# Two ranks of a planner changed in the opening of an attention and mixing kernel: evacuations of batch 0's token units, value products of batch 1

## The chip, the cores and the metric

The kernel runs on one core of a Trainium2 chip. TensorE (PE) multiplies matrices into PSUM banks, VectorE (DVE), ScalarE (ACT) and GpSimd (POOL) work on elements, and SyncE (SP) issues the DMAs between HBM and SBUF. Each engine works through its own instructions in order and waits for others by semaphores. The metric is the device time in microseconds (us).

## The reference

Eight batches, eight heads, 576 positions, head size 64. Attention is windowed: four heads see the last 32 positions, four see every fourth of the last 128. Its output, as rows of 512 channels, is the input x of a second part.

```python
scores = np.where(masks, scale * q @ k.T, -1e9)
attn = exp(scores - max); attn = attn / (sum(attn) + 1e-9)
x = attn @ v                                  # per batch 576 x 512
theta = x @ w_theta
zr, zi = x * cos(theta), x * sin(theta)
y = w_tok_r @ zr + w_tok_i @ zi               # mixes positions
u = x + y
out = u + maximum(u @ w_ch, 0)
```

All is float32. The kernel splits each operand of the large products into a high and a low part and adds three products (high by high, high by low, low by high).

## The kernel before, in words

A batch is done in stages. Heads go in four pairs. `scores` puts a pair's scores into two PSUM banks (tag s, two buffers), adds the mask there by a product with an identity matrix for batch 0 and a few pairs of batches 1 and 2, takes the maxima (L430, DVE), scales them (L438, DVE), lets ACT do the exponentials with their sums (L485) and normalises on POOL (L510). `turn` transposes the probabilities P in eight pieces on DVE (L525) into one of two buffers pt. `pv` multiplies them with the values (L617, tile o), ACT copies the result to x (`x_evac`, L581), and `x_split` makes high and low parts (xh: L593 on ACT, L597 and L599 on DVE, for the last pair on POOL). `theta` multiplies x with w_theta (L685), `trig` makes sines and cosines, and `zsplit` the parts zh and zl. A batch has 16 units of 288 columns: eight `token` units y (27 matmuls, L850, over the nine z tiles in the order of `KORD`) and eight `chan` units c (12 matmuls, L882). A token unit ends in `residual`, which adds it to x (L825, DVE), makes u's high part (L828, ACT) and low part (L830, POOL) and so frees the bank; a channel unit ends in `finish` (L859).

Units of batch b run on PE while batch b+1 goes through attention. The weights come as packed words and are unpacked once, in the opening: clamp (L332, DVE), two steps on ACT (L334, L340), join (L342, DVE), high part (L350, ACT), low part (L352, POOL). The token weights of the second half of the positions (`late_wt_a`, `late_wt_b`) and the channel weights (`late_wc`) come late; a channel weight is loaded into the staging space that an earlier weight leaves when its L352 is done (`LATE2`), and x_split of batch 1 then takes the same spaces.

The order in the opening (batch 0, and batch 1 up to its theta) is dealt out by a small planner, `Order`. Every piece of work is a generator that names an engine and an estimate. `run` picks the engine that can start first, and on it, among the pieces ready by its estimates, the one with the lowest rank:

```python
t = min((t for t in ready if t[4] == eng and t[2] <= at), key=lambda t: (t[0], t[1]))
```

A piece that starts another without a rank hands its own on, so x_evac and x_split of batch 1 run at the rank of their `pv`. `residual` and `finish` are started with a rank of their own, RANK["evacuate"] (L853, L884). Loads have RANK["load"]. The order found is the order of the program; on the chip nothing is reordered. From batch 1's own units on (`phase`) the order is written out by hand and the ranks play no part.

Of the kernel before, what the change touches and what calls it, by code (L numbers as in the profile page):

```python
# [30 lines left out]
LATE = ("u3", "xh1", "xh2", "xh3", "xh0")  # L31
LATE2 = ("xh2", "xh3", "xh2", "xh3")
RANK = dict(load=6.64, scores0=1.09, flip=0.01, pv0=1.13, pair=.21, theta_unpack=1.54, theta0=5.3, trig0=2.41,
            token_early=2.55, theta_split=6.42, token_late=6.75, chan=2.1, units=2.95, evacuate=4.49,
            scores1=4.02, scores2=7.3, pv1=8.0, theta1=5.96, trig1=7.42)
STS = (4, 0, 1, 2, 3)


# [1020 lines left out]
```

## Time and profile before

| | |
|---|---|
| median of 3 runs | 577.86 us (577.52 to 578.83) |
| profiled execution | 577.82 us, of it span 576.0 us |
| mean granted clock of PE | 0.988 |
| busy PE / DVE / ACT / POOL | 550.5 / 378.0 / 345.2 / 222.2 us |
| moved by DMA | 81.91 MB, mean 142 GB/s |

A row of the timeline gives start and length in us, engine, line, operation, tiles, how many instructions it holds, and in brackets the idle time before them with what ended it. A matmul's end is modelled: starts are what to go by. The granted clock of PE is 1.00 at 2.4 GHz and 0.50 at 1.2 GHz; a value between is a mean.

### The profile page before, as it was taken

The page shows a single profiled execution, that of the slowest core. Times are in us where ns is not written, and L with a number is a line of the kernel's source. Part 1 is how long each engine was busy: PE and PEld are TensorE (multiplying, and loading weights), DVE is VectorE, ACT ScalarE, POOL GpSimd, SP SyncE. Part 2 cuts the span into 40 slices and gives each one's busy share as a digit, 9 for nine tenths or more (in the row PEclk, how much of TensorE's full clock was granted, in tenths as well). Part 3 has the DMA queues.
Part 4 walks back from the last instruction along what each step waited for, and adds up shares of the span by engine and source line. Part 5 has one row for each costly group of instructions (what it writes and reads, how often), then busy time and mean ns, then how long its engine had stood idle before and what let it go on. Part 6 is the DMA issues. An engine that isn't in the chain of part 4 may idle for free.

```text
span 576.0 us, 13996 instructions
## 1 busy us (share of the span) xinstructions
PE 550.5 (96%) x5464; PEld 501.6 (87%) x5464; DVE 378.0 (66%) x1156; ACT 345.2 (60%) x939; POOL 222.2 (39%) x206
## 2 busy tenths in 40 slices
PE   5997799999999999999999999999999999999997
PEld 4744688879999899988999899988999899989997
DVE  3879798865666668756776768756775767445112
ACT  1498967768555784369555785359556695266110
POOL 2228855525224352226324253226323353325220
PEclk9999699899999999999999999999999999999999
DMA  8991437601747046540746146550747123321002
GB/s 303 400 368 28 165 105 245 216 0 63 231 150 193 32 162 210 169 127 20 268 143 172 64 148 202 181 136 11 252 146 190 69 83 102 77 89 65 18 1 83
DMA packets 45586, 81.91 MB, mean 142 GB/s; under 512 B 3920, under 2 KB 19024, under 8 KB 45520
## 3 DMA queue, kind: packets, MB, share of 16 engines
q1 hardware_dynamic: 45520, 81.02, 43.7%
q8 instruction: 43, 0.70, 0.5%
q14 instruction: 23, 0.19, 0.1%
HBM read 64.49 MB, written 16.52 MB: 141 GB/s over the span
## 4 chain that ended last, share of the span: by engine, by line
DVE 34%; ACT 30%; PE 25%; issue 5%; POOL 2%; DMA 2%; SPq 0%; ACTq 0%; POOLq 0%; DVEq 0%
DVE pt L525 16%; PE y L850 11%; ACT P L504 11%; PE c L882 6%; PE th L685 3%; DVE P L409 3%; ACT K L698 3%; ACT K L787 3%; DVE xh L599 3%; ACT th L796 2%; ACT zh L644 2%; DVE xq L729 2%; DVE K L789 2%; ACT cos L705 2%; ACT x L581 2%
## 5 line engine op out<-in xcount | busy, mean ns | idle before, releaser
L830 POOL TENSOR_TENSOR u<-x,u 128x288 fp32r<-128x288 f32 x64 | 54.7, 858 | 184.6 <-ACT u L828 184.6
L525 DVE STREAM_TRANSPOSE pt<-P 32x288 f32<-32x288 f32 x224 | 105.1, 469 | 12.0 <-POOL P L510 8.9
L882 PE MATMUL c<-u,late_wc 128*128 128x288 f32 x768 | 110.2, 296 | 2.8 <-DVE x L859 2.8
L882 PEld LDWEIGHTS c<-u,late_wc 128*128 128x128 f32 x768 | 106.0, 188 | 6.8 <-DVE x L859 4.0
L850 PE MATMUL y<-wtkh,zh 128*128 128x288 f32 x288 | 90.3, 314 | 1.1 <-ACT zh L644 1.1
L850 PE MATMUL y<-wtkh,zl 128*128 128x288 f32 x288 | 86.2, 299 | 4.0 <-POOL zl L646 4.0
L646 POOL TENSOR_TENSOR zl<-g,zh 128x512 fp32r<-128x512 f32 x40 | 52.3, 1316 | 97.5 <-ACT zh L644 84.5
L504 ACT ACTIVATE P<-P,mx 128x64 f32<-128x64 f32 x216 | 72.0, 335 | 25.8 <-DVE mx L498 25.8
L850 PE MATMUL y<-wtkl,zh 128*128 128x288 f32 x288 | 85.9, 298 | 0.0
L828 ACT CAST u<-x 128x288 fp32r<-128x288 f32 x64 | 26.9, 429 | 86.2 <-DVE x L825 85.5
L685 PE MATMUL th<-wthh,xh 128*128 128x512 f32 x224 | 74.8, 395 | 0.3 <-DVE g L784 0.3
L850 PE MATMUL y<-late_wt_b,zh 128*128 128x288 f32 x320 | 68.1, 297 | 0.0
L825 DVE TENSOR_TENSOR x<-y,x 128x288 f32<-128x288 f32 x64 | 28.1, 448 | 53.6 <-PE y L850 53.5
L850 PEld LDWEIGHTS y<-wtkh,zl 128*128 128x128 f32 x288 | 55.1, 191 | 4.7 <-POOL zl L646 4.7
L850 PEld LDWEIGHTS y<-wtkh,zh 128*128 128x128 f32 x288 | 54.9, 191 | 4.7 <-ACT zh L644 2.3
L850 PE MATMUL y<-late_wt_a,zh 128*128 128x288 f32 x256 | 56.3, 301 | 0.0
L850 PEld LDWEIGHTS y<-wtkl,zh 128*128 128x128 f32 x288 | 55.1, 191 | 0.3 <-issue 0.3
L510 POOL TENSOR_TENSOR P<-P,sm 128x576 f32<-128x576 f32 x32 | 37.5, 1172 | 41.1 <-DVE sm L508 18.1
L850 PEld LDWEIGHTS y<-late_wt_b,zh 128*128 128x128 f32 x320 | 51.4, 189 | 0.3
L685 PEld LDWEIGHTS th<-wthh,xh 128*128 128x128 f32 x224 | 42.0, 188 | 9.2 <-DVE g L784 0.6
L850 PE MATMUL y<-late_wt_b,zl 128*128 128x288 f32 x160 | 47.4, 296 | 0.0
L581 ACT COPY x<-o 128x576 f32<-128x576 f32 x32 | 29.4, 919 | 28.4 <-PE o L617 19.1
(108 smaller groups left out, 1106.3 us busy)
## 6 DMA issues: line engine op xcount, KB each, us to landing
q<-in_qT_dram SPq DMA_DIRECT2D x32, 576.0 KB, 5.2
va<-in_vw_dram SPq DMA_DIRECT2D x30, 320.0 KB, 3.2
k<-in_kT_dram SPq DMA_DIRECT2D x28, 304.0 KB, 5.5
out_dram<-x SPq DMA_DIRECT2D x28, 288.0 KB, 2.4
vb<-in_vw_dram SPq DMA_DIRECT2D x29, 256.0 KB, 3.8
xd<-xq SPq DMA_DIRECT2D x24, 288.0 KB, 5.1
xn<-xd SPq DMA_DIRECT2D x24, 256.0 KB, 3.4
st_wtk<-in_wtk_dram SPq DMA_DIRECT2D x8, 576.0 KB, 8.8
```

Of the source, the lines that this page charges most:

```text
L409: pin(nc.vector.tensor_tensor_reduce(out=P[:, n], in0=ps[:, n - g0], in1=mskb[:, mask_of(pr, n)], op0=ALU.add, op1=ALU.max, scale=1.0, sca ...
L504: table(nc.scalar.activation(P[:, n], P[:, n], AF.Exp, bias=mx[:, n:n + 1], scale=SCALE, accum_out=sm[:, n:n + 1]))
L510: pin(nc.gpsimd.tensor_tensor(P, P, sm.unsqueeze(2).to_broadcast([128, NJ, BW]), op=ALU.mult))
L525: pin(nc.vector.transpose(pmats[b, pr][k0:k0 + QB, :, hh, QB * e:QB * e + QB], P[p0:p0 + QB, :, QB * o:QB * o + QB]))
L581: pin(nc.scalar.copy(dst, src))
L646: pin(nc.gpsimd.tensor_tensor(lo, z, hi.bitcast(F32), op=ALU.subtract))
L685: pe(nc.tensor.matmul(pt, l, r, start=(n == 0), stop=(n == 3 * NC - 1)))
L825: pin(nc.vector.tensor_tensor(x[:, ts], ps, x[:, ts], op=ALU.add))
L828: pin(nc.scalar.copy(uh[b, d][:, ts], x[:, ts]))
L830: pin(nc.gpsimd.tensor_tensor(ul[b, d][:, ts], x[:, ts], uh[b, d][:, ts].bitcast(F32), op=ALU.subtract))
L850: pe(nc.tensor.matmul(ps, l[:, cs], r, start=(n == 0), stop=(n == 3 * NK - 1)))
L882: pe(nc.tensor.matmul(ps, l[:, cs], r[:, ts], start=(n == 0), stop=(n == 3 * NC - 1)))
```

## The change

The rank of evacuations falls from 4.49 to 1.49: below sines and cosines (2.41 and 7.42), units (2.95), channel weights (2.1) and all scores after batch 0's. The rank of batch 1's value products falls from 8.0 (plus 0.21 per pair) to 5.0: below theta of batch 1 (5.96), the late token weights (6.75) and the scores of batch 2 (7.3).

```diff
--- before.py
+++ after.py
@@ -31,8 +31,8 @@
 LATE = ("u3", "xh1", "xh2", "xh3", "xh0")
 LATE2 = ("xh2", "xh3", "xh2", "xh3")
 RANK = dict(load=6.64, scores0=1.09, flip=0.01, pv0=1.13, pair=.21, theta_unpack=1.54, theta0=5.3, trig0=2.41,
-            token_early=2.55, theta_split=6.42, token_late=6.75, chan=2.1, units=2.95, evacuate=4.49,
-            scores1=4.02, scores2=7.3, pv1=8.0, theta1=5.96, trig1=7.42)
+            token_early=2.55, theta_split=6.42, token_late=6.75, chan=2.1, units=2.95, evacuate=1.49,
+            scores1=4.02, scores2=7.3, pv1=5.0, theta1=5.96, trig1=7.42)
 STS = (4, 0, 1, 2, 3)
 
 
```

No instruction is added or taken away. The order is the same on every engine up to the middle of token unit y0_2_0 of batch 0 (74 us in the trace), and again from early in the theta of batch 1 on. Names: y0_1_1 is batch 0's token unit for channels 128 to 255 and the second half of the positions, o1_3 the value product of batch 1's pair 3, s2_1_0 the first part of the scores of batch 2's pair 1, pt1 the turned probabilities that o1_3 reads.

PE where the value product of pair 3 stands, before:

```order
L850 MATMUL y0_2_1_1297<-late_wt_a_802,zh0_3_795 128x288 x2
L850 MATMUL y0_2_1_1297<-late_wt_a_802,zl0_3_796 128x288
L850 MATMUL y0_2_1_1297<-late_wt_b_1008,zh0_7_754 128x288 x2
L850 MATMUL y0_2_1_1297<-late_wt_b_1008,zl0_7_755 128x288
L617 MATMUL o1_3_1341<-pt1_109,va1_3_1110 64x64 x10
L617 MATMUL o1_3_1341<-pt1_109,vb1_3_1260 64x64 x8
L850 MATMUL y0_2_1_1297<-late_wt_b_1008,zh0_8_581 128x288 x2
L850 MATMUL y0_2_1_1297<-late_wt_b_1008,zl0_8_582 128x288
L850 MATMUL y0_3_1_1411<-late_wt_a_802,zh0_0_612 128x288 x2
L850 MATMUL y0_3_1_1411<-late_wt_a_802,zl0_0_613 128x288
```

It stood near the end of token unit y0_2_1, behind the scores of pair (2,1). The same product in the changed kernel:

```order
L850 MATMUL y0_1_1_1235<-late_wt_b_936,zh0_7_754 128x288 x2
L850 MATMUL y0_1_1_1235<-late_wt_b_936,zl0_7_755 128x288
L850 MATMUL y0_1_1_1235<-late_wt_b_936,zh0_8_581 128x288 x2
L850 MATMUL y0_1_1_1235<-late_wt_b_936,zl0_8_582 128x288
L617 MATMUL o1_3_1291<-pt1_109,va1_3_1124 64x64 x10
L617 MATMUL o1_3_1291<-pt1_109,vb1_3_1227 64x64 x8
L850 MATMUL y0_2_1_1302<-late_wt_a_802,zh0_0_612 128x288 x2
L850 MATMUL y0_2_1_1302<-late_wt_a_802,zl0_0_613 128x288
L850 MATMUL y0_2_1_1302<-late_wt_b_936,zh0_4_576 128x288 x2
L850 MATMUL y0_2_1_1302<-late_wt_b_936,zl0_4_577 128x288
L424 LDWEIGHTS idb_94
L424 MATMUL s2_1_0_1333<-mskb_93,idb_94 128x64
```

It now stands right behind token unit y0_1_1, ahead of all of y0_2_1 and of the scores of pair (2,1).

DVE around the turn of the pair that this product reads (the transposes into pt1), before:

```order
L597 TENSOR_TENSOR xh1_0_1133<-x1_0_903,xh1_0_1133 128x64
L525 STREAM_TRANSPOSE pt1_109<-P1_3_968 32x9x32 x2
L342 SCALAR_TENSOR_TENSOR st_wch1_1113<-st_wch1_1113 128x512
L525 STREAM_TRANSPOSE pt1_109<-P1_3_968 32x9x32 x2
L430 TENSOR_REDUCE mx2_0_1166<-s2_0_0_1168 128x5
L525 STREAM_TRANSPOSE pt1_109<-P1_3_968 32x9x32 x2
L438 TENSOR_SCALAR mx2_0_1166<-mx2_0_1166 128x5
L525 STREAM_TRANSPOSE pt1_109<-P1_3_968 32x9x32 x2
L430 TENSOR_REDUCE mx2_0_1166<-s2_0_5_1203 128x4
L599 TENSOR_TENSOR xh1_0_1133<-x1_0_903,xh1_0_1133 128x512
```

One join of a channel weight and the maxima of batch 2's first scores stood between the pieces. In the changed kernel:

```order
L599 TENSOR_TENSOR xh1_1_1162<-x1_1_1060,xh1_1_1162 128x512
L430 TENSOR_REDUCE mx2_0_1158<-s2_0_0_1160 128x5
L342 SCALAR_TENSOR_TENSOR st_wch1_1088<-st_wch1_1088 128x512
L525 STREAM_TRANSPOSE pt1_109<-P1_3_992 32x9x32 x2
L597 TENSOR_TENSOR xh1_0_1204<-x1_0_897,xh1_0_1204 128x64
L525 STREAM_TRANSPOSE pt1_109<-P1_3_992 32x9x32 x2
L825 TENSOR_TENSOR x0_0_274<-y0_0_1_1100,x0_0_274 128x288
L332 TENSOR_SCALAR st_wch2_1170<-st_wch2_1170 128x512
L525 STREAM_TRANSPOSE pt1_109<-P1_3_992 32x9x32 x2
L599 TENSOR_TENSOR xh1_0_1204<-x1_0_897,xh1_0_1204 128x512
L342 SCALAR_TENSOR_TENSOR st_wch2_1170<-st_wch2_1170 128x512
L525 STREAM_TRANSPOSE pt1_109<-P1_3_992 32x9x32 x2
```

The pieces now have the clamp and the join of the third channel weight, the parts of xh1_0 and an evacuation between them, and the scaling of the maxima comes behind the last.

POOL around the last piece of the late token weights (late_wt_b from st_wtk1_4), before:

```order
L510 TENSOR_TENSOR P1_2_905<-P1_2_905,sm1_2_907 128x576
L352 TENSOR_TENSOR late_wt_b_1008<-st_wtk1_3_479,late_wt_b_1008 128x576
L352 TENSOR_TENSOR late_wt_b_1008<-st_wtk1_4_698,late_wt_b_1008 128x288
L830 TENSOR_TENSOR u0_3_1121<-x0_3_476,u0_3_1121 128x288
L510 TENSOR_TENSOR P1_3_968<-P1_3_968,sm1_3_970 128x576
L830 TENSOR_TENSOR u0_0_831<-x0_0_274,u0_0_831 128x288
```

It followed the piece before it. In the changed kernel:

```order
L352 TENSOR_TENSOR late_wt_b_936<-st_wtk1_3_479,late_wt_b_936 128x576
L830 TENSOR_TENSOR u0_3_1101<-x0_3_476,u0_3_1101 128x288
L352 TENSOR_TENSOR late_wc0_1134<-st_wch0_961,late_wc0_1134 128x512
L510 TENSOR_TENSOR P1_3_992<-P1_3_992,sm1_3_994 128x576
L352 TENSOR_TENSOR late_wt_b_936<-st_wtk1_4_698,late_wt_b_936 128x288
L352 TENSOR_TENSOR late_wc1_1207<-st_wch1_1088,late_wc1_1207 128x512
```

An evacuation's low part, the first channel weight and the normalisation of P of pair 3 now stand in front of it.

## Rows read from the trace of the kernel before

**Rows 1.** Busy time of the engines, page, part 1.

```profile
PE 550.5 (96%) x5464; PEld 501.6 (87%) x5464; DVE 378.0 (66%) x1156; ACT 345.2 (60%) x939; POOL 222.2 (39%) x206
```

**Rows 2.** Windows: busy time of PE, PEld, DVE, ACT, POOL; PEclk, DMA, GB/s.

```profile
75.00:99.00 24.00, 22.95 (x331) 20.39 (x330) 21.43 (x48) 16.74 (x57) 12.97 (x12) 1.00 0.58 196
102.00:105.00 3.00, 3.00 (x28) 2.61 (x26) 2.19 (x8) 2.19 (x10) 1.25 (x1) 0.50 0.81 257
105.00:106.00 1.00, 1.00 (x10) 0.72 (x10) 0.61 (x3) 0.18 (x1) 0.00 (x0) 0.82 0.97 380
...
126.00:200.00 74.00, 74.00 (x709) 68.86 (x708) 48.31 (x162) 46.70 (x129) 27.83 (x26) 1.00 0.43 130
```

**Rows 3.** Timeline of PE: start, length, instruction, count, idle before it.

```profile
82.47 0.31 PE L424 MATMUL s<-mskb,idb 128*128 128x64 bf16 x5 [1.04 <-ACT P L485]
...
88.42 0.43 PE L850 MATMUL y<-late_wt_a,zh 128*128 128x288 f32 x2
88.68 0.30 PE L850 MATMUL y<-late_wt_a,zl 128*128 128x288 f32 x1
...
95.71 0.80 PE L617 MATMUL o<-pt,va 128*64 128x64 f32 x20
...
101.51 0.30 PE L424 MATMUL s<-mskb,idb 128*128 128x64 bf16 x2 [1.95 <-ACT P L485]
...
107.86 0.80 PE L617 MATMUL o<-pt,va 128*64 128x64 f32 x20
...
120.27 0.49 PE L685 MATMUL th<-wthh,xh 128*128 128x512 f32 x1 [0.33 <-DVE g L784]
...
125.11 0.63 PE L759 MATMUL xn<-idt,x 128*128 128x128 f32 x4 [1.02 <-DVE g L750]
```

**Rows 4.** Groups of DVE, 86 to 112 us: busy us, mean ns, idle before.

```profile
L525 DVE STREAM_TRANSPOSE pt<-P 32x288 f32<-32x288 f32 x22 | 10.3, 469 | 0.4
L342 DVE SCALAR_TENSOR_TENSOR st_wch<-st_wch 128x512 uint32<-128x512 uint32 x4 | 2.9, 736 | 0.1
L332 DVE TENSOR_SCALAR st_wch<-st_wch 128x512 f32<-128x512 f32 x4 | 2.3, 571 | 1.6 <-DMA st_wch<-in_wch_dram 1.5
L825 DVE TENSOR_TENSOR x<-y,x 128x288 f32<-128x288 f32 x4 | 1.8, 452 | 0.5 <-PE y L850 0.5
...
L599 DVE TENSOR_TENSOR xh<-x,xh 128x512 fp32r<-128x512 f32 x2 | 1.4, 691 | 0.0
...
L430 DVE TENSOR_REDUCE mx<-s 128x5 f32<-128x320 f32 x2 | 1.0, 493 | 0.1
...
L597 DVE TENSOR_TENSOR xh<-x,xh 128x64 fp32r<-128x64 f32 x2 | 0.4, 215 | 0.0
```

**Rows 5.** Timeline of DVE.

```profile
80.54 0.17 DVE L438 TENSOR_SCALAR mx<-mx 128x5 f32<-128x5 f32 x1
...
84.77 1.30 DVE L438 TENSOR_SCALAR mx<-mx 128x5 f32<-128x5 f32 x1
...
86.43 0.75 DVE L438 TENSOR_SCALAR mx<-mx 128x4 f32<-128x4 f32 x1
...
91.07 0.43 DVE L332 TENSOR_SCALAR st_wch<-st_wch 128x512 f32<-128x512 f32 x1
91.53 0.96 DVE L525 STREAM_TRANSPOSE pt<-P 32x288 f32<-32x288 f32 x2
```

**Rows 6.** Timeline of POOL.

```profile
84.60 1.45 POOL L352 TENSOR_TENSOR late_wt_b<-st_wtk,late_wt_b 128x576 fp32r<-128x576 f32 x1 [0.76 <-ACT late_wt_b L350]
86.00 1.15 POOL L510 TENSOR_TENSOR P<-P,sm 128x576 f32<-128x576 f32 x1
...
90.27 0.81 POOL L830 TENSOR_TENSOR u<-x,u 128x288 fp32r<-128x288 f32 x1 [0.94 <-ACT u L828]
```

**Rows 7.** Group of POOL, 72 to 118 us.

```profile
L352 POOL TENSOR_TENSOR late_wc<-st_wch,late_wc 128x512 fp32r<-128x512 f32 x4 | 5.5, 1385 | 2.6 <-ACT late_wc L350 2.6
```

**Rows 8.** DMA issues, 60 to 125 us: count, KB each, median us to landing.

```profile
vb<-in_vw_dram SPq DMA_DIRECT2D x4, 256.0 KB, 5.4
```

## The prediction

> **What bounds the kernel now.** I read the busy times of the page first: TensorE (PE) works 550.5 of 576.0 us [rows 1], so only time in which PE idles or runs at its lower clock can be won or lost. The windows [rows 2] then say where that is: from 126 us to 200 us PE is busy all the time at full clock. What the change moves lies between 74 and 143 us (the order of every engine is the same up to 74 us and, names apart, again from early in batch 1's theta on), so whatever delay PE has when this stretch ends goes into the time in full. The timeline of PE [rows 3] names the waits in it: 1.04 us before 82.47 and 1.95 us before 101.51 (both: a score bank held until ScalarE's exponentials are done), 0.33 at 120.27 and 1.02 at 125.11 (both: the theta chain on VectorE). After the idle 1.95 us the granted clock is 0.50, that is 1.2 GHz, for 102 to 105 and part of 105 to 106: a mean of 0.82 in that last us means 0.36 us at half. So 3.36 us at half clock, in which 1.68 us of work are lost [rows 2]. After the wait of 1.04 it stays at 2.4 GHz (1.00 over 75 to 99), and it is there again from 126 on [rows 2, 3]. Together PE loses 1.04 + 1.95 + 0.33 + 1.02 + 1.68 = 6.02 us. The change can win no more than that here.
>
> The profiled execution took 577.82 us, its span 576.0 with 1.8 around it; the median of the runs is 577.86, so the sum below is made on 577.8 and needs no shift. From about 0.2%, 1.2 us, a difference can be told from none.
>
> **The change part by part.** No instruction is added or removed (DVE's two more rows are runs that print apart); two ranks change, and the planner deals out a new order. Times below are on the clock of the trace.
>
> *First wait (82.47).* PE's score matmuls of pair (1,2) now come six token matmuls earlier. On VectorE the scaling of their maxima (L438) stands behind two transposes fewer (2 x 0.47) and one L342 more (0.74) [rows 4], so it ends 0.2 us earlier, and the exponentials behind it too. But PE comes to the bank three token matmuls sooner: the two of the row at 88.42 and the next begin 0.26 apart, so 0.13 each, 0.40 for three [rows 3]. The wait becomes 1.04 + 0.40 - 0.24 = 1.20. Unit y0_1 starts at 88.6 instead of 88.42.
>
> *Value product of pair 2 (o1_2) and the last late weights.* PE comes to o1_2 at about 92.9 instead of 95.71 [rows 3]: 24 y matmuls (3.2) and about half of batch 2's first scores with their masks (1.1: before, the 7.3 us from 88.42 to 95.71 held 39 y matmuls, 5.1, and all of them). It needs the turned P of pair 2. Before, that turn ended at 91.53 + 0.96 = 92.5 [rows 5]. Now one L342 more stands in front of its end (0.7), y0_3's evacuation no longer makes VectorE wait (0.5, the idle time of L825 in [rows 4]), and the scores come 0.1 sooner: 92.6. Bounds: 92.2, if VectorE is held less there than before, and 94.5 if the first channel weight's L332, now in front of the maxima of pair 3, is caught by GpSimd. What shows that price is L438 at 84.77: 1.30 us, ending with GpSimd's L352 (84.60 to 86.05), and at 86.43: 0.75 us, ending with the L510 after it; undisturbed such a scaling takes 0.17 (80.54 in [rows 5]). The weights themselves are no wait: their slot is free when GpSimd has done the first piece of late_wt_b, which now is at 80 (L342 ends near 77.8, cast and product take 2.1), and a load on this queue takes 5.4 us or less [rows 8], so it lands by 85.4, and VectorE comes to it near 84.7: what it may wait is inside the bounds.
> The last piece of late_wt_b is a new wait. On GpSimd it stood right behind its forerunners, and PE never waited for it; now u0_3 (0.8, at about 90.4; before at 90.27), a channel weight (1.39) and P of pair 3 (1.15) run ahead of it [rows 6, 7], and with its own 0.8 (half as long as the piece at 84.60) it is done at about 94.6. PE wants it after o1_2 (1.2 us), at 94.1: 0.5 us. Between 0 and 1.3.
>
> *Value product of pair 3 (o1_3), the main term.* Before it stood 24 y matmuls and the scores of pair (2,1) later, at 107.86 [rows 3]. Now PE comes to it right behind y1_1. The work up to there is what PE did before from 88.42 to 99.56 (101.51 less the idle 1.95) without a wait, less three y matmuls: 99.3 with the 0.16 from above, 99.8 with the 0.5.
> It needs the turn of pair 3 on VectorE, eight transposes. Between the turn of pair 2 and the end of this one the changed queue has two L332, two L342, two L597, two L599, one L430 and one L825 as well. At the means of the stretch [rows 4]: 8 x 0.469 + 2 x 0.571 + 2 x 0.736 + 2 x 0.215 + 2 x 0.691 + 0.493 + 0.452 = 9.1 us. From 92.6 that is 101.7, with GpSimd in the way no more than it is on average. Yet GpSimd now runs from 90.4 to 94.6 without a gap, and its product for the second channel weight starts when VectorE's L342 for the same weight ends, two transposes ahead of an L597: both times VectorE comes with an instruction of the kind that was held. Two holds cost (1.30 - 0.17) + (0.75 - 0.17) = 1.7 us at 84.77 and 86.43 [rows 5, 6]. I take these two: 103.4, a wait of 3.6 us. Bounds: 101.0 (turn of pair 2 at 92.2, L332 at its undisturbed 0.43 [rows 5], no hold) and 105.3 (94.5 + 9.1 + 1.7).
> On the price of a hold the Trainium skill speaks against this change: "SBUF — State Buffer", section "Who interferes with whom", has VectorE and GpSimd share a port pair which the one that issues first keeps for its whole instruction while the other "fully blocks", tensor_scalar and two-input VectorE instructions among them. The trace agrees (1.30 us, ending with GpSimd's 1.45). By that rule a third L597 hold would count in full as well, 0.8 more, and the sum would be 580.3; by the means alone it would be 577.7.
>
> *Clock.* The new wait is longer than the 1.95 us that took the clock to 1.2 GHz before. I price it as that one: 1.68 us. Bounds: 0, if the wait stays near the 1.04 that cost none, and 3.4, a stretch at half clock twice as long.
>
> *Theta.* The waits of 0.33 and 1.02 come from the addition L784, which stood behind eight transposes of pair (2,1); now it stands behind two, so much of them goes; but GpSimd's work for that pair also comes later. 0.75 remains, between 0 and 1.35.
>
> *Cover.* The other moved steps (casts on ScalarE, loads on SP's queue) are hidden by the wait before o1_3. The second half of pair 2's values is such a load: it follows o1_1 on the queue, so it is issued near 89.3, and took 5.4 us before [rows 8], with two channel weights close in front of it; now one of them runs 6 us sooner. It lands between 93 and 94.7, where o1_2 wants it at 93.5. What it adds there PE would wait at o1_3 otherwise. With that cover gone (A below) it costs up to 1.2 us.
>
> **Sum.** 1.20 + 0.5 + 3.6 + 1.68 + 0.75 = 7.7 against 6.0: 1.7 us more, 579.5 us. From 126 us on PE has no slack in which that could be given back [rows 2].
>
> **The rivals.**
> *A, faster: VectorE is in time and the clock holds.* Place: o1_3. Without a hold it starts at 101.0, PE came at 99.3, and a wait of 1.7, between the 1.04 that kept the clock and the 1.95 that lost it, may keep it. Loss 1.20 + 1.7 + 0.2 = 3.1, so 2.9 less than before: 574.9 (576.6 if the clock does fall). It decides at a start of about 101.9: with the clock lost, the sum is 6.0 there. For it: L332 on its own takes 0.43. Against: GpSimd has no gap there. 13%.
> *B, no difference.* Holds as in the mean, start at 101.7: 1.20 + 0.5 + 1.9 + 1.68 + 0.6 = 5.9, 577.7 us. For it: these means have holds in them already. With starts between 101 and 103 around it, 27%.
> *C, much slower.* The chain of maxima, exponentials and sums is held twice before the turn of pair 2, which ends at 94.5: o1_2 waits 1.6, o1_3 until 105.3 (PE there at 101.3: 4.0), and the clock is lost for twice as long: 1.20 + 1.6 + 0.4 + 4.0 + 3.4 + 0.75 = 11.4, 583.2 us. For it: L332 now comes to the port at the moment in which P of pair 2 is ready for GpSimd, 84.6. Against: the bank waits of batch 2's scores have 2 us of air. 15%.
> The forecast has 45%, with a range of its own from 578.5 to 581.5.
>
> **How the numbers follow.** Faster by over 0.2%: A, 13%. Within it: B, 27%. Slower: forecast and C, 60%. The range goes from 576.6 (most of A lies below) to 582.6 (most of C lies above).
>
> **What would show it.** In the changed trace PE should idle 3 to 4 us just before o1_3, near 100 to 103.5, put down to VectorE's transposes; the granted clock should be 0.50 after it; the wait before 101.51 for the scores of batch 2 should be gone, as they come later; the wait before 82.47 should still be there at 1.1 to 1.3. L332 and L597 near 93 and 98 should take about 1 us each. It is wrong if o1_3 starts before 102, if PE waits longest elsewhere, or if PE has idle time after 126 us that takes the delay up.

## The result, and the profile after

The changed kernel takes 579.53 us (median of 22 runs, 577.69 to 583.07), the kernel before 578.03 us beside it (22 runs, 575.68 to 579.68): ratio 1.0033, 95% interval 1.0021 to 1.0046. That is 1.5 us slower; 579.5 us and 1.7 more were predicted. The profiled execution of the change took 579.39 us, its span is 577.6.

Executions differ before the change has any say. So the two traces are compared from the last product of batch 0's token units that stands in front of every moved instruction; it is the last row at which the two timelines of PE still run alike, and is called the common product below. Before:

```profile
74.38 0.29 PE L850 MATMUL y<-wtkh,zl 128*128 128x288 f32 x1
```

After, the same product, and below it the waits of PE until theta, with the idle time in brackets:

```profile
74.09 0.29 PE L850 MATMUL y<-wtkh,zl 128*128 128x288 f32 x1
...
82.04 0.31 PE L424 MATMUL s<-mskb,idb 128*128 128x64 bf16 x5 [1.28 <-ACT P L485]
...
93.93 0.69 PE L617 MATMUL o<-pt,vb 128*64 128x64 f32 x16 [0.27 <-DMA vb<-in_vw_dram]
...
103.05 1.22 PE L617 MATMUL o<-pt,va 128*64 128x64 f32 x17 [3.20 <-DVE pt L525]
...
126.81 0.63 PE L759 MATMUL xn<-idt,x 128*128 128x128 f32 x4 [0.58 <-DVE g L750]
```

From the common product to the end of the span the kernel before needs 576.0 - 74.38 = 501.62 us, the change 577.6 - 74.09 = 503.51: 1.89 more. The waits answer to [rows 3]: 1.28 for 1.04 at the first bank, 0.58 in place of 0.33 and 1.02 in theta, no wait for batch 2's scores where there were 1.95, and 3.20 us before o1_3 (L617, put down to VectorE's transposes), which did not wait before.

Busy times change little; this row of the page answers to [rows 1]:

```profile
PE 551.3 (95%) x5464; PEld 502.7 (87%) x5464; DVE 379.5 (66%) x1156; ACT 345.3 (60%) x939; POOL 220.9 (38%) x206
```

The windows of the change (length, PE busy, PEclk, DMA share, GB/s) answer to [rows 2]:

```profile
99.00:102.00 3.00, 0.85 (x7) 0.94 0.86 303
102.00:105.00 3.00, 1.95 (x34) 0.50 0.08 31
105.00:108.00 3.00, 3.00 (x17) 0.50 0.62 197
108.00:110.00 2.00, 2.00 (x28) 0.88 0.00 0
110.00:114.00 4.00, 4.00 (x42) 1.00 0.15 20
```

The clock falls to 1.2 GHz during the wait (a mean of 0.94 over 99 to 102 puts the fall at about 101.6) and stays there to about 108.5 (0.88 over 108 to 110). VectorE between the turns of pairs 2 and 3, to set beside [rows 5]:

```profile
91.04 0.96 DVE L525 STREAM_TRANSPOSE pt<-P 32x288 f32<-32x288 f32 x2
92.57 0.84 DVE L332 TENSOR_SCALAR st_wch<-st_wch 128x512 f32<-128x512 f32 x1 [0.56 <-DMA st_wch<-in_wch_dram]
93.33 0.83 DVE L597 TENSOR_TENSOR xh<-x,xh 128x64 fp32r<-128x64 f32 x1
...
96.64 1.29 DVE L597 TENSOR_TENSOR xh<-x,xh 128x64 fp32r<-128x64 f32 x1
...
99.30 0.42 DVE L332 TENSOR_SCALAR st_wch<-st_wch 128x512 f32<-128x512 f32 x1
...
102.04 0.96 DVE L525 STREAM_TRANSPOSE pt<-P 32x288 f32<-32x288 f32 x2
103.03 1.05 DVE L438 TENSOR_SCALAR mx<-mx 128x5 f32<-128x5 f32 x1
```

The last two transposes of pair 2 end at 92.0, those of pair 3 at 103.0; before it was 92.5 and, by its timeline, 99.87 + 0.96 = 100.8. So the stretch from the one end to the other takes 11.0 us for 8.3, and with the 0.3 us between the common products the turn of pair 3 ends 2.5 us later. L332 takes 0.84 us here and 0.42 at 99.30; L597 takes 1.29 where [rows 4] have a mean of 0.215. GpSimd in the same time, beside [rows 6]:

```profile
90.69 1.32 POOL L352 TENSOR_TENSOR late_wc<-st_wch,late_wc 128x512 fp32r<-128x512 f32 x1
91.96 1.16 POOL L510 TENSOR_TENSOR P<-P,sm 128x576 f32<-128x576 f32 x1
93.07 1.00 POOL L352 TENSOR_TENSOR late_wt_b<-st_wtk,late_wt_b 128x288 fp32r<-128x288 f32 x1
96.53 1.32 POOL L352 TENSOR_TENSOR late_wc<-st_wch,late_wc 128x512 fp32r<-128x512 f32 x1 [2.45 <-ACT late_wc L350]
```

L597 at 96.64 ends at 97.93, with the product of the channel weight that began at 96.53. I call such a lengthening (the prediction's hold) **stretching**: what an instruction takes beyond the shortest of its kind.

### The profile page after: what moved, and what is told of

It is laid out like the page before. It is cut to its first block, busy times and chain, and to the rows that moved or that the text cites. A ratio compares the mean times of both kernels' runs of the same rounds, so it can differ in the third digit from the quotient of the medians.

```text
span 577.6 us, 13996 instructions
## 1 busy us (share of the span) xinstructions
PE 551.3 (95%) x5464; PEld 502.7 (87%) x5464; DVE 379.5 (66%) x1156; ACT 345.3 (60%) x939; POOL 220.9 (38%) x206
## 4 chain that ended last, share of the span: by engine, by line
PE 37%; DVE 30%; ACT 23%; DMA 5%; issue 3%; POOL 2%; SPq 0%; POOLq 0%; ACTq 0%; DVEq 0%
PE y L850 16%; DVE pt L525 13%; ACT P L504 8%; PE c L882 8%; PE th L685 5%; DMA st_wtk<-in_wtk_dram 3%; DVE P L409 3%; PE s L468 3%; ACT K L698 2%; PE o L617 2%; DVE xh L599 2%; ACT K L787 2%; ACT th L796 2%; POOL P L510 2%; DVE K L789 2%
## 5 line engine op out<-in xcount | busy, mean ns | idle before, releaser
L825 DVE TENSOR_TENSOR x<-y,x 128x288 f32<-128x288 f32 x64 | 28.2, 449 | 53.6 <-PE y L850 53.4
L581 ACT COPY x<-o 128x576 f32<-128x576 f32 x32 | 29.3, 917 | 28.2 <-PE o L617 23.5
## 6 DMA issues: line engine op xcount, KB each, us to landing
q<-in_qT_dram SPq DMA_DIRECT2D x32, 576.0 KB, 5.0
st_wtk<-in_wtk_dram SPq DMA_DIRECT2D x8, 576.0 KB, 8.8
```

The lines of the kernel that those rows point to most:

```text
L581: pin(nc.scalar.copy(dst, src))
L825: pin(nc.vector.tensor_tensor(x[:, ts], ps, x[:, ts], op=ALU.add))
```

## The experiments

Theory 1, with which I went in: the price is the place of o1_3, which stands ahead of unit y0_2 now. Theory 2: the evacuations' rank costs it, wherever PE then waits. All ratios below are to runs of the kernel before that were made beside them; the change has 1.0033. Each trace is of one execution: those of e2_pv_alone and e9_no_chan_low are the fastest of twelve runs, those of e5_warm, e7_split_late, f2_before_no_chan_low and f3_evac_3 the slowest of theirs.

**One half of the change alone.**

```diff
 e1_evac_alone: evacuate=4.49 -> 1.49, pv1 stays 8.0
 e2_pv_alone:   pv1=8.0 -> 5.0, evacuate stays 4.49
```

> Only the evacuations' rank is changed (evacuate 4.49 to 1.49), the value products keep theirs. Theory 1 (the price is the place of o1_3: TensorE comes to the value product of pair 3 before VectorE has turned it): o1_3 stands 24 or more y matmuls later again, behind the scores of pair (2,1), so the 3.20 us before it go, the wait for a score bank before them (1.95 us in the kernel before) returns in part, with the clock at half after it; 577.0 to 578.3 us, within 0.2% of before. Theory 2 (the evacuations' rank costs it, because it puts u units and a channel weight ahead of the last late weights on GpSimd, and the wait at o1_3 is only where the delay shows): 579 to 580 us, as the whole change.

> Only the value products' rank is changed (pv1 8.0 to 5.0), the evacuations keep theirs. o1_3 then stands within y0_2_1, 14 y matmuls (1.9 us) later than with the whole change. Theory 1: TensorE still comes too early, but by less: a wait of 1.0 to 2.5 us at o1_3 and the bank wait of the scores of batch 2 gone; the time is between before and the whole change, 577.5 to 579.3 us. Theory 2 (evacuations cost it): no loss against before, 577.5 to 578.2 us, and no wait over 1 us at o1_3.

Evacuations alone: 580.10 us, 1.0026 (1.0007 to 1.0045). Value products alone: 577.21 us, 0.9991 (0.9974 to 1.0008). With the evacuations alone o1_3 stands late again and does not wait, and yet the time is that of the whole change. PE's longer waits in that trace, but for the first (0.67 us):

```profile
102.11 0.30 PE L424 MATMUL s<-mskb,idb 128*128 128x64 bf16 x2 [3.42 <-ACT P L485]
...
121.63 1.06 PE L882 MATMUL c<-u,late_wc 128*128 128x288 f32 x6 [1.10 <-DVE x L859]
...
127.05 0.63 PE L759 MATMUL xn<-idt,x 128*128 128x128 f32 x4 [0.83 <-DVE g L750]
```

The 3.4 us now stand before the scores of batch 2 (1.95 before). Theory 1 missed here: it had 578.3 us at most and less than 1.95 us of this wait. Theory 2 had 579 to 580 us. In the second kernel, too, o1_3 does not wait, and the bank wait is still there (2.49 us): theory 1, which had 1.0 to 2.5 us at o1_3 and no bank wait, misses again, and theory 2 had no loss (577.5 to 578.2 us).

**o1_3 taken back, all else as in the change.**

```diff
@@ pv(b, pr)
+        if (b, pr) == (1, 3):
+            yield None, ("tk", 0, 2, 1)
```

> The whole change, but the value product of pair 3 is held until y0_2_1 is done, so it stands 26 y matmuls and the first scores of pair (2,1) later (3.4 us and 1.1 us); VectorE's and GpSimd's order up to the turn of pair 3 stay as with the change. Theory 1: the 3.20 us go, and the half clock behind them (2.7 us) goes or is bought again by a bank wait before the second half of the scores of pair (2,1); 574.5 to 577.5 us, faster than the change by 2 us or more. Theory 2: the evacuations' delay is there whatever PE waits for, so the same time as the change within 0.5 us, 579 to 580 us, with a wait of some 3 us elsewhere between 95 and 110.

580.70 us, 1.0053 (1.0030 to 1.0076): theory 1 expected it at 577.5 or less, and falls; theory 2 had 579 to 580 and some 3 us of waits elsewhere. PE's longer waits:

```profile
95.35 0.69 PE L619 MATMUL o<-pt,vb 128*64 128x64 f32 x16 [1.67 <-DMA vb<-in_vw_dram]
...
106.27 0.30 PE L424 MATMUL s<-mskb,idb 128*128 128x64 bf16 x2 [1.77 <-ACT P L485]
...
126.75 0.63 PE L761 MATMUL xn<-idt,x 128*128 128x128 f32 x4 [0.89 <-DVE g L752]
```

The 3.20 us are gone, and 1.77 for a score bank and 1.67 for the second half of pair 2's values have come, 3.4 together. That load was issued no later than in the change, as the rows of SP's queue show (issue time, time that the issue took). The change, then this kernel:

```profile
88.38 0.34 SPq L250 DMA_DIRECT2D vb<-in_vw_dram  x1
```

```profile
88.41 0.34 SPq L250 DMA_DIRECT2D vb<-in_vw_dram  x1
```

PE stops waiting for it at 93.93 in the one and at 95.35 in the other: 5.6 and 6.9 us after the issue.

In the place of theory 1 came theory V: VectorE's queue sets the end of this stretch, and PE waits for it wherever it stands. Beside it stood theory L, the loads, and theory H, a form of V: VectorE is late because GpSimd stretches its instructions.

**Channel weights behind the turns, and x's splitting behind the turns.** Both take work of VectorE out of the turn of pair 3.

```diff
 e4_chan_behind_turn: chan=2.1 -> 4.9
 e7_split_late:
-            go(x_split(b, pr))
+            go(x_split(b, pr), 8.0 + pr * RANK["pair"] if b == 1 else None)
```

> The whole change, and the channel weights of batch 1 rank behind the turns (chan 2.1 to 4.9). The turn of pair 3 sheds one L597 (1.29 us in the changed trace, held by GpSimd), one L599 (0.69) and one L342 (0.69) and takes one L438 (0.2): 2.5 us; o1_3 stands 6 y matmuls (0.8 us) earlier. Theory 1: a wait of 3.20 - 2.5 + 0.8 = 1.5 us at o1_3, half clock for at most as long as in the kernel before; 576.5 to 578.5 us. Theory 2: the evacuations stand where the change puts them, 579 to 580 us.

> The changed kernel with the splitting of batch 1's x (x_split) ranked behind the turns, at 8.0 and up as it was before the change; in the change it went forward with the value products, whose rank it takes over. Between the turns of pairs 2 and 3 VectorE sheds one L597 (1.29 us) and one L599 (0.69) and has two L438 and one L430 more (0.8); o1_3 stands 3 y matmuls (0.4 us) earlier. Theory V: the turn of pair 3 ends about 1.2 us earlier, the maxima and exponentials of batch 2's first scores, of which o1_3's wait has none, 2 us and more earlier; 577.5 to 579.0 us. If the evacuations' own steps are what costs (first channel weight's L332 in front of the maxima of pair 3), it stays at 579 to 580.

583.35 us, 1.0081 (1.0052 to 1.0111), and 583.17 us, 1.0083 (1.0064 to 1.0102). Both expectations miss: the gain by 4 us and more, the 579 to 580 of the other case by over 3. The rows of VectorE in the first of them show a part of why:

```profile
92.24 1.07 DVE L507 TENSOR_SCALAR sm<-sm 128x9 f32<-128x9 f32 x1
...
93.77 1.18 DVE L597 TENSOR_TENSOR xh<-x,xh 128x64 fp32r<-128x64 f32 x1
94.87 1.31 DVE L599 TENSOR_TENSOR xh<-x,xh 128x512 fp32r<-128x512 f32 x1
...
98.08 1.22 DVE L438 TENSOR_SCALAR mx<-mx 128x5 f32<-128x5 f32 x1
```

An L597, an L599 and an L342 are out of the turn, but others are stretched in their place: L507 takes 1.07 for 0.17, L597 1.18 for 0.21, L599 1.31 for 0.69, L438 1.22 for 0.17. The turn of pair 3 ends no earlier (29.0 us behind the common product, 28.9 in the change). PE then waits in theta, where the change had 0.58 us; in the second kernel it waits before batch 0's channel products, and its clock is at 0.50 a second time, from 124 to 127 us. The first kernel, then the second:

```profile
127.91 0.63 PE L759 MATMUL xn<-idt,x 128*128 128x128 f32 x4 [1.91 <-DVE g L750]
```

```profile
123.73 0.99 PE L882 MATMUL c<-u,late_wc 128*128 128x288 f32 x3 [1.88 <-DVE x L825]
```

**The clock held up.** The 24 products are extra work.

```diff
@@ pv(b, pr), ahead of the products of o1_3
+        for _ in range(24 if (b, pr) == (1, 3) and od.live else 0):
+            pe(nc.tensor.matmul(ps[:, :HS], zs[0, 0][0][:, :128], wtks[0, 0][0][:, :HS],
+                                start=True, stop=True))
```

> The changed kernel with 24 products added in TensorE's queue right before o1_3 (128x288, of weights and sines that are long there; they write o1_3's bank, which o1_3 overwrites, so nothing reads them); every other engine's order stays. At 0.13 us each they fill the wait of 3.2 us. If the clock costs what the trace says (5.4 us at half, 2.7 us lost), o1_3 starts where it did, at 103, with no idle time before it, the granted clock stays 1.00 over 99 to 110, and the time is 2 to 2.7 us below the change: 576.8 to 577.6 us. If the half clock were not brought on by the wait, or gave work back later, the time stays within 0.5 us of the change.

580.39 us, 1.0041 (1.0024 to 1.0058): nothing is won, where 576.8 to 577.6 us were expected. The clock did what was expected:

```profile
99.00:102.00 3.00, 3.00 (x25) 1.00 0.81 268
102.00:105.00 3.00, 3.00 (x25) 1.00 0.78 260
105.00:108.00 3.00, 2.53 (x45) 1.00 0.13 51
108.00:110.00 2.00, 1.53 (x22) 1.00 0.90 288
```

In the change these windows had 0.94, 0.50, 0.50 and 0.88. But PE at full clock comes to the next banks before they are free, and to the channel products before VectorE:

```profile
106.29 0.74 PE L620 MATMUL o<-pt,va 128*64 128x64 f32 x17 [0.47 <-DVE pt L525]
...
108.25 0.29 PE L853 MATMUL y<-late_wt_b,zl 128*128 128x288 f32 x1
109.00 0.30 PE L424 MATMUL s<-mskb,idb 128*128 128x64 bf16 x2 [0.47 <-ACT P L485]
...
112.72 0.29 PE L853 MATMUL y<-late_wt_b,zl 128*128 128x288 f32 x1
113.22 0.27 PE L424 MATMUL s<-mskb,idb 128*128 128x256 bf16 x1 [0.20 <-ACT P L485]
...
123.76 0.53 PE L885 MATMUL c<-u,late_wc 128*128 128x288 f32 x2 [0.44 <-DVE x L862]
```

The same token products in the change, in front of the two masks:

```profile
106.53 0.44 PE L850 MATMUL y<-late_wt_b,zl 128*128 128x288 f32 x1
...
111.25 0.29 PE L850 MATMUL y<-late_wt_b,zl 128*128 128x288 f32 x1
```

By starts alone, from o1_3's main part to the last token product in front of the first mask it takes 108.25 - 106.29 = 1.96 us here and 106.53 - 103.05 = 3.48 in the change; from that mask to the last one in front of the second, 112.72 - 109.00 = 3.72 against 111.25 - 106.77 = 4.48 (the first mask of the change is at 106.77 in its timeline). So the half clock costs PE 1.52 + 0.76 = 2.28 us, and 0.47 + 0.20 + 0.44 = 1.11 of it come back as waits. (In this execution o1_3 also began 0.6 us later than in the change, 29.56 us behind the common product for 28.96: two L332 took 1.36 and 1.30 us in it, the change's first two 0.40 and 0.84. And the 24 products take 3.25 us by their starts, 102.24 to 105.49, as long as the wait in the change's trace: where VectorE is earlier they themselves keep o1_3 back. How much of the missing gain is theirs was not measured.)

**The load of pair 2's second half left out.**

```diff
@@ load_vb(n)
-            vb = ap.tile([128, NJ - VA, 128], F32, tag="vb", name=f"vb{b}_{pr}", bufs=1)
+            vb = ap.tile([128, NJ - VA, 128], F32, tag="vb", name=f"vb{b}_{pr}", bufs=1) \
+                if (b, pr) != (1, 2) else vs["b", 1, 1][0]
         yield "DMA", dma((NJ - VA) * 128)
-        pin(nc.sync.dma_start(vb, vw[b, pr, :, VA:]))
+        if (b, pr) != (1, 2):
+            pin(nc.sync.dma_start(vb, vw[b, pr, :, VA:]))
```

> The changed kernel without the load of the second half of pair (1,2)'s values; o1_2 reads pair (1,1)'s half in its place, so the value products of that pair come from other data. No other instruction moves. Theory L (the loads that stand behind o1_1 on the queue are what differs between executions: in the profile of the change it landed 5.3 us after its issue and cost 0.27 us, in that of the kernel with pair 3 late 6.9 us and 1.67, with the clock lost behind it): the waits before o1_2 and for the first L332 behind the turn of pair 2 are gone, the executions lie closer together, under 3 us where the change has 5.4, and the median falls by 0.5 to 1.5 us, to 578.0 to 579.0. Theory V (VectorE's queue alone sets the end of this stretch): the wait of 0.27 moves to o1_3, the same time as the change within 0.4 us, and the same spread.

580.36 us, 1.0038 (1.0022 to 1.0054), where theory L had 578.0 to 579.0; the 8 runs lie from 578.97 to 581.81. The median is no lower, so the load does not set it; the runs are too few to judge the spread. PE's wait before o1_3:

```profile
103.39 1.22 PE L619 MATMUL o<-pt,va 128*64 128x64 f32 x17 [3.70 <-DVE pt L527]
```

3.70 in place of 3.20: what PE no longer waits for the load it waits here, as VectorE's turn ends no earlier (o1_3 starts 28.95 us behind the common product for 28.96).

**GpSimd's products beside VectorE left out, in the change and in the kernel before.** This pair tests theory H: the kernels leave out the low part of two channel weights, so that GpSimd does nothing where these products stood.

```diff
@@ chan_weights(c, stage)
+        if c < 2:
+            wchs[c] = (t[:, :DM], t[:, :DM])
@@ split(T, sz, dst, key)
-        pin(nc.gpsimd.tensor_tensor(lo, T, hi.bitcast(F32), op=ALU.subtract))
+        if key not in (("wch", 0), ("wch", 1)):
+            pin(nc.gpsimd.tensor_tensor(lo, T, hi.bitcast(F32), op=ALU.subtract))
```

> The changed kernel without GpSimd's product (L352, 1.32 us each) for the first two channel weights; their high half is read where the low half was, so the channel products lose the low part. All other queues stay. Theory V with holds: L332 at 92.57 (0.84 us) falls to 0.43, L597 at 93.33 (0.83) and at 96.64 (1.29) fall to 0.2, so the turn of pair 3 ends 2.0 us earlier, o1_3 waits 1.0 to 1.5 in place of 3.20 us, and the clock falls for a shorter stretch or not at all: 575.0 to 577.5 us. If the holds are not what makes VectorE late (something else fills the time), o1_3 waits as long as before, 579 to 580 us.

> The kernel before without GpSimd's products (L352) for the first two channel weights, whose high half is read where the low half was: the same cut as in the kernel without channel low halves, but made in the kernel before. Theory H (the change is slower because it puts GpSimd's products beside those instructions of VectorE that a product of GpSimd stretches: 4.3 us of stretching in the changed trace up to 29 us behind the last common product, 2.5 in that of before): here the two products run at 96.73 beside transposes, which keep their 0.95 us, so nothing is won, 577.6 to 578.5 us, and between the two kernels without these products 0.6 us at most remain of the 1.5. Rival (any work taken off GpSimd helps either kernel alike): 1.0 to 1.6 us faster than before.

The change without them: 578.61 us, 1.0006 (0.9990 to 1.0021). The kernel before without them: 578.54 us, 1.0010 (0.9996 to 1.0025). Without the two products the change loses 0.0027 of its ratio, 1.6 us (0.9 by the medians), and the interval just touches that of the change; the kernel before wins nothing, and between the two cut kernels no difference is left (578.61 and 578.54 us). So the change costs 0.0033 with the products and -0.0004 without; the difference of 0.0037 is uncertain by about 0.0025, an estimate from the three intervals. The rival, that any work taken off GpSimd helps either kernel alike, had the kernel before 1.0 to 1.6 us faster, and falls. In the kernel before this is where they ran, beside transposes and steps that kept their length:

```profile
96.73 2.86 POOL L352 TENSOR_TENSOR late_wc<-st_wch,late_wc 128x512 fp32r<-128x512 f32 x2 [0.33 <-ACT late_wc L350]
```

```profile
97.18 0.96 DVE L525 STREAM_TRANSPOSE pt<-P 32x288 f32<-32x288 f32 x2
...
98.69 0.95 DVE L525 STREAM_TRANSPOSE pt<-P 32x288 f32<-32x288 f32 x2
```

In the change without the two products VectorE's rows are short again:

```profile
92.36 0.43 DVE L332 TENSOR_SCALAR st_wch<-st_wch 128x512 f32<-128x512 f32 x1 [0.89 <-DMA st_wch<-in_wch_dram]
92.70 0.22 DVE L600 TENSOR_TENSOR xh<-x,xh 128x64 fp32r<-128x64 f32 x1
...
95.66 0.23 DVE L600 TENSOR_TENSOR xh<-x,xh 128x64 fp32r<-128x64 f32 x1
...
100.00 0.96 DVE L528 STREAM_TRANSPOSE pt<-P 32x288 f32<-32x288 f32 x2
```

From the end of pair 2's turn to the end of pair 3's VectorE takes 9.5 us for the change's 11.0: the three stretched rows are 2.1 us shorter, and it idles 0.5 us more. The first product worked by pushing others back: in the change the L332 of 92.57 and the L597 of 93.33 stand beside the normalisation and the late weight that GpSimd does behind it (91.96 and 93.07); without it both are done by 92.5. PE's wait before o1_3 is 1.32 us, with the clock at 1.00 in every window from 96 to 110 us:

```profile
101.02 0.74 PE L620 MATMUL o<-pt,va 128*64 128x64 f32 x17 [1.32 <-DVE pt L528]
```

The rows did much of what was expected (2.0 us off the turn of pair 3; it was 1.5), the time did not: 577.5 us at most, a gain of 2 to 4.5, was expected in the change, and 578.61 misses it. Here too PE met new waits (0.46, 0.16 and 0.45 us). This trace is of the fastest run, 576.6 us; in the median run less was won than it shows.

**Two more orders, and the value products once more.**

```diff
 f3_evac_3:    evacuate=1.49 -> 3.5 (pv1=5.0)
 f4_pv_front:  pv1=4.3, evacuate=4.49
 e2b_pv_alone: as e2_pv_alone
```

> The changed kernel with the evacuations' rank at 3.5 in place of 1.49: still in front of the attention of batch 1, but behind the sines, the channel weights and the units. u0_3 and the first channel weight change places on GpSimd, two instructions of SP as well, and VectorE's order round the turn of pair 3 changes (o1_3 3 y matmuls earlier). If passing the sines and channel weights is what costs, 577.5 to 578.5 us; if it is the passing of the attention, 579 to 580.5 us, and by theory H the stretching of VectorE's instructions stays at 4 us or more. I expect the second.

> The kernel before with the value products' rank at 4.3, in front of the evacuations' 4.49, which keep theirs. A try at a version better than both: value products early as in the one-part kernel that read 577.21, and still further in front. By theory H it is as good as that one if its stretching stays under 2 us (576.8 to 577.8 us); over 4 us of stretching goes with 579 and more.

> The value products' rank alone (5.0) once more, for a second interval on whether this half of the change is faster than before: by the first runs 0.9991 with 0.9974 to 1.0008. Theory H expects it at or just under before, 577.0 to 578.0 us, as its trace has 1.7 us of stretching where before has 2.5.

581.35 us, 1.0061 (1.0039 to 1.0082); 579.37 us, 1.0029 (1.0016 to 1.0042); 577.57 us, 0.9998 (0.9985 to 1.0011). The first is above the 579 to 580.5 that was expected, the third as expected; the second, with 3.24 us of stretching in the table below, lies between the two cases of its expectation. So what costs is that evacuations pass the attention; value products put in front of them cost as well; the value products' half as it stands in the change makes no difference, with both intervals around 1. No order that I tried beats the kernel before.

All traces together, in the order of the stretching. It is the sum over L332, L342, L438, L507, L597 and L599 of duration less the shortest of its kind (0.43, 0.69, 0.17, 0.17, 0.21, 0.69; 0.76 for L342 with 576 columns), where that is 0.2 or more, from the product common to all orders (column "from") to 29 us behind it, about where the turn of pair 3 ends; it is from one execution each. "Turn end" is the end of that turn behind "from"; the last two columns are PE's idle time, and its busy time at half clock, in the 72 us behind "from":

```
kernel                  from   span - from  stretching  ratio to before  turn end  idle  half
e2_pv_alone             73.33  501.17       1.44        0.9991           26.7      3.94  3.4
e2b_pv_alone            75.30  500.70       1.45        0.9998           26.1      4.76  0
e9_no_chan_low          73.55  501.25       1.87        1.0006           27.4      4.88  0
e3_pair3_late           74.05  504.25       2.06        1.0053           29.4      5.69  6.8
f2_before_no_chan_low   77.11  500.89       2.08        1.0010           25.6      3.51  3.4
before                  74.38  501.62       2.28        1                26.5      4.35  3.4
f4_pv_front             74.57  502.33       3.24        1.0029           32.7      5.70  0
after                   74.09  503.51       3.97        1.0033           28.9      5.33  5.4
e1_evac_alone           75.10  503.10       3.99        1.0026           28.2      6.04  3.4
e4_chan_behind_turn     74.40  506.10       4.06        1.0081           29.0      7.22  5.5
e6_no_vb                74.44  503.66       4.13        1.0038           28.9      5.56  5.5
e7_split_late           75.75  506.85       4.20        1.0083           28.7      6.35  9.2
f3_evac_3               76.27  504.93       4.26        1.0061           29.9      6.45  4.7
e5_warm                 76.73  503.47       4.76        1.0041           29.5      3.55  0
```

Under 2.3 us of stretching the time is that of before, above 3.2 it is 0.26 to 0.83% longer, with one exception: in e3_pair3_late VectorE waited 1.81 us for a late channel weight and met fewer of GpSimd's products for it. The end of the turn has no exception: up to 27.4 us the time is that of before, from 28.2 on it is longer. In e3 the load made VectorE late, so stretching is one way to be late and not the only one. How much a kernel loses follows from neither column, but from PE's own: take the idle time off "span - from", and 0.42 us for each busy us at half clock (an estimate: 2.28 us, by the run with the clock held up, over the 5.4 of the change), and in that run the 24 products; 495.6 to 496.7 us are left in all 14. (f4_pv_front moves even the products around this place, so its "from" and turn end are worth less.)

## Why the prediction was right, and which of its reasons was not

The number and the sign were right, the place of the long wait too. That the number is so close is in part luck: the wait at o1_3 and the last weight, in whose place a shorter wait came, were priced 0.6 us too high together, the clock 0.6 too low. Step by step:

*First wait:* 1.20 predicted, 1.28 measured.

*The last piece of late_wt_b:* 0.5 predicted, none measured. On GpSimd it ended at 93.07 + 1.00 = 94.07, half a microsecond before the 94.6 of the prediction, and PE took it without a wait behind o1_2. What came in its place is the load that the part "Cover" priced at up to 1.2: 0.27 us. (The prediction read the 5.4 us of [rows 8], a median, as the most that a load takes; PE waited for this one until 5.6 us after its issue, in another run until 6.9.) The run without that load shows its price to be nothing, since PE waits the same time at o1_3.

*o1_3:* a wait of 3.6 and a start at 103.4 were predicted, 3.20 and 103.05 measured. The turn of pair 2 ended at 92.0 for 92.6. For the two holds that I took, 1.13 and 0.58 us, VectorE's rows between the turns show three: 0.84 - 0.43, 0.83 - 0.21 and 1.29 - 0.21, together 2.1 us for 1.7. The Trainium skill ("SBUF — State Buffer", "Who interferes with whom") lets a VectorE instruction with at most one input in SBUF and outside the two-port modes run beside GpSimd, and has one with two inputs in SBUF contend with a GpSimd instruction that reads SBUF. The trace agrees as far as it goes: the transposes keep 0.94 to 0.96 us for two whatever GpSimd does, L597 with its two inputs goes from 0.22 to 1.29.

*Clock:* 1.68 was priced, as for the wait of 1.95. The half clock lasted 5.4 us of busy time for 3.4, and by the comparison with the run that kept the clock it cost PE 2.28. This term was mis-sized, and two steps behind it failed. It was added to the waits in full, but the kernel with the clock held up was no faster: of what PE gained it waited 1.11 us again, for VectorE and ScalarE. And it took the length of a wait as what decides: the clock also fell behind a wait of 1.67 us (e3_pair3_late, 0.50 from 98 to 100 us), and in two runs it stayed at 1.00 through longer ones. These are in e2b_pv_alone and in f4_pv_front:

```profile
104.17 0.30 PE L424 MATMUL s<-mskb,idb 128*128 128x64 bf16 x2 [2.23 <-ACT P L485]
```

```profile
107.27 0.74 PE L617 MATMUL o<-pt,va 128*64 128x64 f32 x17 [2.38 <-DVE pt L525]
```

What decides it stays open.

*Theta:* 0.75 predicted, 0.58 measured.

*The sum:* 1.28 + 0.27 + 3.20 + 2.28 + 0.58 = 7.61 against 6.02, so 1.6 more; the traces differ by 1.89 over this stretch. The 0.3 that are missing lie about where the prediction took half of the time at half clock as lost: at 0.42 of it, as above, the 3.4 us of the kernel before cost 1.43 for 1.68, and the difference is 1.84. That is an estimate; the clock was held up in the changed kernel alone.

*The reason that failed* is the one under "Value product of pair 3": that the price comes from PE reaching o1_3 early. With o1_3 back behind y0_2 the time stayed at 1.0053, and with the evacuations alone, where o1_3 is late too, at 1.0026. The wait is only where VectorE's lateness shows, and PE's order cannot pay for it. What makes VectorE late is in the step after it: its queue, which I had as the 9.1 us between the turns, and the holds, which I had as 1.7 us of a term. Of the 2.7 us by which the stretch between the ends of the two turns grew, 1.5 are holds (2.1 for the 0.57 of one L332 before), the other 1.1 instructions that did not stand there before. Evacuations in front of the attention let GpSimd take units, channel weights and late weights at the moments when VectorE runs scalings, splits and channel weights; before, the channel products of 96.73 to 99.6 us cost VectorE nothing. Leaving out these two products supports it: no effect seen before, the difference gone after, and the turn of pair 3 earlier by 1.5 us. How much each of the other stretched instructions counts stays open; so does why pulling splits or channel weights out of the turn made PE wait longer later on, at theta and at the channel products, where these two kernels lose much of the 3 us by which they are slower than the change.

The rivals A, B and C rested on the end of the turn of pair 3: 101.0, 101.7 and 105.3; it was 103.0. Without the two products o1_3 started at 101.02 - 73.55 = 27.5 us behind the common product, in the change at 29.0, and the clock stayed up, as A had it; but the gain of 2.9 on the kernel before that A promised did not come (1.0006).

## What to carry to other kernels

A wait of the bounding engine told here where lateness shows, not where it is made: move the waiting instruction away, and if the time stays, look for the engine that was late. When an order is changed, look at which instructions of VectorE meet GpSimd's products: two-input and scaling instructions of 0.2 us took 0.8 to 1.4 us beside them, transposes lost nothing. Terms that lie one behind the other on two engines that wait for each other need not add up: with the clock held up, half of the 2.28 us came back here as waits. An account of PE's idle time and time at half clock, trace by trace, showed where each order lost.

## What was not expected of the hardware

The first 74 us, in which no order differs, end anywhere between 73.3 and 77.1 us in the 13 executions whose "from" can be compared, a range of 3.8 us beside the 4 to 5 us between the runs of one kernel. A load with the same issue time and the same queue in front of it came 5.6 us after its issue in one execution and 6.9 in another. At half clock the 34 products of o1_3's main part with the five token products behind them took 3.48 us for 1.96 by their starts, 1.78 times and not 2. And a wait of 2.38 us left the clock at 1.00, where waits of 1.67 and 1.95 in other traces went with a fall to 0.50.
